# Mamba-2 scan and SwiGLU feed-forward: weight parts by ScalarE and VectorE instead of transfers and GpSimd, and a new step order

## The chip, the core and the metric

The kernel runs on one core of a Trainium2 chip. The core has TensorE (matrix products, "PE" in the profile; its weight loads are "PEld"), VectorE ("DVE"), ScalarE ("ACT"), GpSimd ("POOL") and SyncE ("SP", which here issues nearly all transfers). The metric is device time in microseconds (us), the median of several runs.

## The reference

A scan over the sequence (Mamba-2, in chunks) gives y; y is then the input of a feed-forward block with RMS norm, a gate and a value product, and an output product.

```python
# x (4, 8, 768, 32), a (4, 8, 768), B and C (4, 8, 768, 16), float32
for c in range(768 // 32):
    cum = np.cumsum(np.log(a_c), axis=-1)
    L = np.exp(cum[:, :, :, None] - cum[:, :, None, :]) * causal
    y_intra = ((C_c @ B_c.T) * L) @ x_c
    y_inter = (C_c @ state) * np.exp(cum)
    state = np.exp(cum_last) * state + (B_c * decay_from_j).T @ x_c
x = y.transpose(0, 2, 1, 3).reshape(3072, 256)
xn = x / np.sqrt(np.mean(x * x, -1) + 1e-6) * rms_g
g, v = xn @ w_gate, xn @ w_val        # (256, 1536), float64 inputs
return (g * sigmoid(g) * v) @ w_out   # (1536, 256)
```

## The kernel before

The 3072 tokens are six blocks of 512 (block 0 to 5; the number ahead of the colon in a step's name). The 1536 hidden columns are twelve tiles f of 128, six pairs j of 256. For each block the kernel computes the scan, normalises its output, makes the gate and value products for each f, the SwiGLU, and the output products.

**Weights.** The three weight matrices arrive as 64-bit words and are turned into float32 on the chip, in 20 pieces. Pieces 0 to 13 are gate and value columns (0 to 3 are 128 columns wide, the others 256; even is gate, odd is value; 4 and 5 are pair 1, 6 and 7 pair 2, and so on), pieces 14 to 19 are w_out, two tiles f each. A piece k goes through fetch.k (transfer, SyncE, into one of six buffers "wr"), pow.k, powk.k, powe.k (exponent, three ScalarE instructions, L164, L170, L179), man.k, mane.k (mantissa, VectorE, L186, L194) and wt.k (VectorE, L200).

**Split products.** Six tiles f of block 0 (early, gate) are multiplied in plain float32 straight from the tiles whole_w (columns 0 to 767). All else of gate and value uses a split: every weight tile is cut into a leading part (top, the upper bits), a difference s = ONE * top - w and a trailing part m = w - top, and the normalised input likewise (xm, xs, xl, xh). Step sw.j.k makes top (VectorE, L819) for pair j and k = 0 gate, 1 value; sws.j.k makes s (VectorE, L924); swm.j.k makes m (L929). A product then has three steps: D.f.k (s by xs, L941), W.f.k (ScalarE scales the sum in PSUM, L945), and G.f.k (leading part by xh and trailing part by xl, L952). SiLU is L957 (block 0: silug.f), the product with the value L960 (hidg.f).

**Where the leading parts lie before.** In one tile wgv for all columns. For pairs 0 to 2, step keep.k copies a whole piece from whole_w into wgv by a transfer issued by SyncE (L207); later sw reads it there, and step kt.j.k overwrites it with the top tile, again by a transfer (L934). For pairs 3 to 5 only kt.j.k is needed. The tiles whole_w share their place with the s tiles of pairs 3 to 5.

**Order.** Nothing is scheduled at run time. A list of some 1,530 steps is written out in the code; each step issues its instructions to the engines' queues, and each engine works through its own queue in order. So the list fixes the order on every engine, and a waiting instruction holds up those behind it. Names used below: a, aT, la0 (the decays' start), idle.7 (seven warm-up products), mask, sums, exp (the decay matrices of block 0), L, y.p (scan output of token pair p, 256 tokens), yt.p and sq.p (its copies and squares, ScalarE), 1:S.p (states of the next pair, VectorE), turn (transposes), o.f (output product of block 0), early.f.s (plain products of token half s), gate.f (plain products of all tokens), hid.f (their SwiGLU), a slash and a number (the PSUM pair that a step takes), switch.s (hands PSUM pair s to the split products: s = 1 value, s = 0 gate), rowout and rowe (row sums stored to DRAM).

Of the kernel before, what the change touches and what calls it, by code (L numbers as in the profile page):

```python
# [9 lines left out]
FP32 = mybir.dt.float32  # L10
FP32R = mybir.dt.float32r
# [5 lines left out]
ALU = mybir.AluOpType  # L17
# [4 lines left out]
def kernel(  # L22
# [22 lines left out]
    DM, DF = moe_w_gate.shape  # L45
# [69 lines left out]
    wgv = const.tile([P, 2, 2, DF], FP32R, name="wgv")  # L115
    wgvf = wgv.bitcast(FP32)
    whole_w = [const.tile([P, 2, 2, 256], FP32, tag="sw%d" % (j + NF // 4), name="whole_w")
               for j in range(NF // 4)]

    def whole(n, c, w):  # L120
        return whole_w[c // 256][:, "gv".index(n), :, c % 256:c % 256 + w]
# [82 lines left out]

    def keep(k):
        n, c, w = pieces[k]
        nc.sync.dma_start(out=wgvf[:, "gv".index(n), :, c:c + w], in_=whole(n, c, w))  # L207
# [690 lines left out]
    def split_w(j, k):  # L898
        if j not in Sw:
            if j < NF // 4:  # L900
                Sw[j] = raw.tile([P, 2, 2, 256], FP32R, tag="wr", name="sw", bufs=6)
            else:
                Sw[j] = const.tile([P, 2, 2, 256], FP32R, tag="sw%d" % j, name="sw%d" % j)
# [12 lines left out]
        w = parts.pop((2 + 2 * j + k, "w")) if j >= 3 else wgvf[:, k, :, 256 * j:256 * j + 256]  # L916
# [10 lines left out]
    def trailing_w(j, k):  # L927
        w, s, m = splits[j, k]
        nc.gpsimd.tensor_tensor(out=m, in0=w, in1=tops[j, k], op=ALU.subtract)  # L929
# [3 lines left out]
    def keep_top(j, k):  # L933
        nc.sync.dma_start(out=wgvf[:, k, :, 256 * j:256 * j + 256], in_=tops[j, k])  # L934

    GV = {}
# [11 lines left out]
    def main_gv(blk, f, k):  # L948
        for t in range(2):
            for lhsT, rhs in ((wgv[:, k, t, f * P:(f + 1) * P], xh[blk][:, t]),  # L950
# [180 lines left out]
    def by_vector(out, in_, scale):  # L1131
# [39 lines left out]
        "hidg": lambda f: hide_gv(0, f), "keep": keep, "kt": keep_top,  # L1171
# [15 lines left out]
    def of_chunk(n, fn):  # L1187
# [28 lines left out]
        0:fetch.2 0:set 0:ones 0:zeros 0:upto 0:a 0:ident 0:mid 0:warm 0:whole 0:fetch.0 0:idle.7  # L1216
        0:ident16 0:never 0:whole16 0:mask.0.0/0 0:after 0:bc.0 0:aT 0:bc.1 0:kinks 0:pow.2 0:mids
        0:never16 0:man.2 0:fetch.5 0:after2 0:la0 0:log4.0.4 0:log 0:part 0:part2 0:hmask 0:upto2
        0:mask.1.1/2 0:x.0 0:r.0 0:mean 0:c*2 0:pow.0 0:powk.0 0:tmask 0:mask.0.1/1 0:head 0:sel
        0:turn.0.1 0:parts.0 0:sums.0.1 0:middles 0:turn.0.0 0:cx 0:sums.0.0 0:d 0:exp.0.1 0:T.0.1  # L1220
        0:Tt.0.1.1 0:Tt.0.0.1 0:turn.1.1 0:exp.0.0 0:dx 0:powe.0 0:x.1 0:Tt.0.0.0 0:sums.1.1 0:T.1.1
        0:Tt.1.0.1 0:T.0.0 0:Tt.0.1.0 0:Tt.1.1.1 0:man.0 0:exp.1.1 0:mane.0 0:g.0.1/1 0:turn.1.0
        0:cc 0:scale.1 0:last.1 0:fetch.1 0:Tl.1 0:Tt.1.0.0 0:scale.0 0:L.0.1 0:gcol 0:wt.0
        0:g.0.0/0 0:L.0.0 0:last.0 0:man.5 0:fetch.6 0:mask.1.0/1 0:Tt.1.1.0 0:sums.1.0 0:A.0
        0:powk.2 0:S.0 0:fetch.4 0:row.1 0:T.1.0 0:g.1.0/2 0:A.1 0:Tl.0 0:row.0 0:mane.5 0:g.1.1/0
        0:fetch.9 0:rowout.1 0:pow.5 0:y.0/1 0:mane.2 0:exp.1.0 0:fetch.3 0:L.1.0 0:rowe.1 0:S.1
        0:powk.5 0:L.1.1 0:log4.4.2 0:powe.5 0:wt.5 0:keep.5 0:log4.6.2 0:r.1 0:keep.0 0:powe.2
# [172 lines left out]
```

## Time and profile before

| what | us |
|---|---|
| median of 3 runs | 407.91 |
| lowest and highest | 407.06, 409.32 |
| the profiled execution | 409.15 |
| its span, first to last instruction | 407.4 |
| TensorE busy | 386.8 |
| VectorE busy | 250.2 |
| ScalarE busy | 242.4 |
| GpSimd busy | 59.2 |
| bytes moved by DMA | 31.69 MB |

The mean granted TensorE clock was 0.987 of full speed. "Busy" is the union of an engine's instruction times; a matmul's end is modelled, and a waiting engine counts as idle. A line such as L952 is a line of the kernel's code. In the timeline and the groups, a bracket or the last column gives the idle time just before an instruction and what ended it.

### The profile page before, as it was taken

Reading aid. Unit: us, or ns where it says so; the run is one execution under the profiler, and the core shown is the slowest. Engines: PE = TensorE matmul, PEld = TensorE weight load, DVE = VectorE, ACT = ScalarE, POOL = GpSimd, SP = SyncE. Lnnn points to the kernel's source line nnn. Section 1 sums busy time; section 2 is a strip of 40 time slices with the busy share of each in tenths; the row PEclk is TensorE's granted clock in tenths of the full one; section 3 lists DMA queues with packets and bytes.
Section 4 is the critical chain, followed back from the end, with each engine's and each line's share of the span. In section 5 each row is a group of like instructions: output and inputs, shape, how many; then the busy total and the mean of one; then the engine's idle time right before and its main releaser. Section 6 shows DMA issues by size and latency. Waiting matters only on the chain.

```text
span 407.4 us, 9256 instructions
## 1 busy us (share of the span) xinstructions
PE 386.8 (95%) x3749; PEld 315.5 (77%) x3749; DVE 250.2 (61%) x533; ACT 242.4 (60%) x441; POOL 59.2 (15%) x69
## 2 busy tenths in 40 slices
PE   6999977969999899999999999899999999999997
PEld 4656345648778689987879988689988889988897
DVE  5899989979971447972267643247815158424542
ACT  3899757656768356466773465766575563365530
POOL 3110604123205011120110120101510010000000
PEclk9999998969999999999999999999999999999999
DMA  9967986916561424601343001311000001100001
GB/s 131 251 126 202 244 158 157 257 65 208 126 90 52 67 49 108 73 2 27 108 78 85 32 9 29 101 43 35 0 27 2 2 2 60 51 0 2 0 2 52
DMA packets 98034, 31.69 MB, mean 78 GB/s; under 512 B 77608, under 2 KB 91816, under 8 KB 97992
## 3 DMA queue, kind: packets, MB, share of 16 engines
q1 hardware_dynamic: 93832, 30.85, 33.1%
q10 hardware_dynamic: 4160, 0.26, 0.8%
q8 instruction: 29, 0.48, 0.5%
q14 instruction: 13, 0.11, 0.1%
HBM read 22.64 MB, written 3.74 MB: 65 GB/s over the span
## 4 chain that ended last, share of the span: by engine, by line
PE 70%; DVE 17%; ACT 6%; issue 5%; DMA 2%; SPq 1%; DVEq 0%; ACTq 0%
PE gv L952 26%; PE o L1022 20%; PE gv L941 13%; PE y L703 3%; DVE S L655 2%; PE o L964 2%; DVE m L194 1%; ACT e L164 1%; DVE sw L924 1%; PE g L566 1%; DMA a_sb<-in_a_dram 1%; DVE top L819 1%; DVE m L186 1%; PE tp L509 1%; DVE h L960 1%
## 5 line engine op out<-in xcount | busy, mean ns | idle before, releaser
L952 PE MATMUL gv<-xh,wgv 128*128 128x512 f32 x264 | 108.0, 409 | 0.4 <-ACT gv L945 0.3
L952 PE MATMUL gv<-xl,mw 128*128 128x512 f32 x264 | 104.7, 397 | 0.0
L960 DVE SCALAR_TENSOR_TENSOR h<-gv,u 128x512 f32<-128x512 f32 x66 | 45.4, 690 | 96.3 <-PE gv L952 82.3
L945 ACT ACTIVATE gv<-gv 128x512 f32<-128x512 f32 x132 | 74.9, 587 | 49.3 <-PE gv L941 49.1
L941 PE MATMUL gv<-xs,sw 128*128 128x512 f32 x264 | 81.3, 411 | 6.4 <-DVE sw L924 2.4
L941 PEld LDWEIGHTS gv<-xs,sw 128*128 128x128 f32 x264 | 47.0, 189 | 18.8 <-issue 3.7
L952 PEld LDWEIGHTS gv<-xh,wgv 128*128 128x128 f32 x264 | 50.2, 190 | 12.4 <-ACT gv L945 1.3
L957 ACT ACTIVATE u<-gv 128x512 f32<-128x512 f32 x66 | 39.3, 600 | 32.1 <-PE gv L952 29.0
L952 PEld LDWEIGHTS gv<-xl,mw 128*128 128x128 f32 x264 | 50.3, 191 | 10.2
L479 POOL TENSOR_SCALAR_AFFINE_SELECT L<-L 64x512 f32<-64x512 f32 x32 | 24.4, 763 | 98.8 <-ACT L L477 97.4
L1022 PE MATMUL o<-wo,h 128*128 128x128 f32 x240 | 33.8, 276 | 0.0
L1022 PE MATMUL o<-two,s 128*128 128x128 f32 x240 | 31.9, 276 | 0.8 <-DVE s L995 0.8
L1022 PEld LDWEIGHTS o<-wo,h 128*128 128x128 f32 x240 | 31.2, 191 | 1.7 <-ACT u L957 0.2
L1022 PEld LDWEIGHTS o<-two,s 128*128 128x128 f32 x240 | 29.7, 192 | 1.8 <-DVE s L995 1.2
L1022 PE MATMUL o<-two,h 128*128 128x128 f32 x240 | 30.1, 275 | 0.0
L1022 PEld LDWEIGHTS o<-two,h 128*128 128x128 f32 x240 | 28.6, 192 | 0.2
L1038 ACT COPY v<-o 128x256 f32<-128x256 f32 x15 | 5.6, 372 | 31.6 <-PE o L1022 31.6
L964 PE MATMUL o<-wo,h 128*128 128x256 f32 x96 | 23.2, 392 | 0.2 <-DVE wo L200 0.2
L753 POOL TENSOR_TENSOR sq<-sq,sq 128x512 f32<-128x512 f32 (+1 forms) x6 | 7.0, 1166 | 109.6 <-issue 70.8
L164 ACT ACTIVATE e<-wr,kinks 128x512 int16<-128x512 int16 (+1 forms) x20 | 14.2, 712 | 13.8 <-DMA wgv<-top 5.3
L964 PEld LDWEIGHTS o<-wo,h 128*128 128x128 f32 x96 | 18.8, 198 | 3.5 <-DVE wo L200 0.6
L1022 PEld LDWEIGHTS o<-wo,s 128*128 128x128 f32 x120 | 15.3, 191 | 0.8
(183 smaller groups left out, 547.4 us busy)
## 6 DMA issues: line engine op xcount, KB each, us to landing
L<-rowd SPq DMA_DIRECT2D x32, 128.0 KB, 3.2
xr<-in_x_dram SPq DMA_DIRECT2D x24, 128.0 KB
wgv<-top SPq DMA_DIRECT2D x12, 256.0 KB, 2.5
wr<-in_moe_w_out_dram SPq DMA_DIRECT2D x6, 512.0 KB, 6.5
wr<-in_moe_w_val_dram SPq DMA_DIRECT2D x5, 512.0 KB
wr<-in_moe_w_gate_dram SPq DMA_DIRECT2D x5, 512.0 KB, 4.9
out_dram<-ob SPq DMA_DIRECT2D x9, 256.0 KB, 2.2
br<-in_B_dram SPq DMA_DIRECT2D x22, 64.0 KB, 2.5
```

The costliest lines, as they stand in the source:

```text
L164: nc.scalar.activation(out=k16, in_=words16, func=AF.Relu, scale=1.0 / 16, bias=kinks[:, 0:1])
L479: nc.gpsimd.affine_select(out=L[r], in_=L[r], pattern=[[0, NH], [1, HC]], compare_op=ALU.is_ge, fill=0.0, base=0, channel_multiplier=-1)
L655: nc.vector.scalar_tensor_tensor(out=S, in0=state[2 * g + u - (2 if p < 2 else 1)], scalar=fcol[:, k:k + 1], in1=new[:, u, i], op0=ALU.mul ...
L703: nc.tensor.matmul(out=y[2 * k + u][rows, (2 * n + i) * HC:(2 * n + i + 1) * HC], start=(k, u, rows.start) not in opened, stop=True, skip_ ...
L753: nc.gpsimd.tensor_tensor(out=sqs[blk][:, tk], in0=sqs[blk][:, tk], in1=sq2, op=ALU.add)
L941: nc.tensor.matmul(out=g, lhsT=Sw[f // 2][:, k, t, (f % 2) * P:(f % 2 + 1) * P], rhs=xs[blk][:, t], start=(t == 0), stop=True, skip_group_ ...
L945: nc.scalar.activation(out=GV[f, k], in_=GV[f, k], func=AF.Copy, scale=-BETA * BETA / (BETA + 1.0))
L952: nc.tensor.matmul(out=GV[f, k], lhsT=lhsT, rhs=rhs, start=False, stop=True, skip_group_check=True)
L957: nc.scalar.activation(out=us[f], in_=GV.pop((f, 0)), func=AF.Silu, scale=ONE)
L960: nc.vector.scalar_tensor_tensor(out=hidden_of(blk, f), in0=GV.pop((f, 1)), scalar=ONE, in1=us.pop(f), op0=ALU.mult, op1=ALU.mult)
L964: nc.tensor.matmul(out=o, lhsT=hs_[blk, f // 2][:, f % 2, k // 2, (k % 2) * P:(k % 2 + 1) * P], rhs=wo[:, f], start=opens, stop=(f == NF - ...
L1022: nc.tensor.matmul(out=o[t] if apart else o[:, t * P:(t + 1) * P], lhsT=lhsT[:, t], rhs=rhs, start=(k in (1, 2, 4, 5) and j == 0 and (apar ...
```

## The change

1. The tile wgv is gone. Each pair j and kind k has a leading-part tile of its own, Gw[j, k], and kt.j.k writes it from top with a ScalarE copy.
2. The eight keep transfers are gone. sw reads pairs 0 to 2 from whole_w itself, whose tiles are now one per j and k and share their place with Gw[j, k] instead of with the s tiles of pairs 3 to 5.
3. swm runs on VectorE instead of GpSimd.
4. The list of steps is in another order, on every engine and in every block. Apart from the eight keep steps the two lists hold the same steps.

```diff
@@ -112,13 +112,11 @@
 
     BETA = 4096.0
     ONE = 1.0 + 1.0 / BETA
-    wgv = const.tile([P, 2, 2, DF], FP32R, name="wgv")
-    wgvf = wgv.bitcast(FP32)
-    whole_w = [const.tile([P, 2, 2, 256], FP32, tag="sw%d" % (j + NF // 4), name="whole_w")
-               for j in range(NF // 4)]
+    whole_w = [[const.tile([P, 2, 256], FP32, tag="g%d%d" % (j, k), name="whole_w")
+                for k in range(2)] for j in range(NF // 4)]
 
     def whole(n, c, w):
-        return whole_w[c // 256][:, "gv".index(n), :, c % 256:c % 256 + w]
+        return whole_w[c // 256]["gv".index(n)][:, :, c % 256:c % 256 + w]
 
     wo = const.tile([P, NF, DM], FP32, name="wo")
 
@@ -201,10 +199,6 @@
                                        in1=e, op0=ALU.mult, op1=ALU.mult)
         if dst is None:
             parts[k, "w"] = f
-
-    def keep(k):
-        n, c, w = pieces[k]
-        nc.sync.dma_start(out=wgvf[:, "gv".index(n), :, c:c + w], in_=whole(n, c, w))
 
     a_sb = ffn.tile([BH, S], FP32, tag="ob", name="a_sb", bufs=1)
     lead16 = ffn.tile([P, 16 * P], BF16, tag="h", name="lead16", bufs=NF // 2)
@@ -900,7 +894,7 @@
             if j < NF // 4:
                 Sw[j] = raw.tile([P, 2, 2, 256], FP32R, tag="wr", name="sw", bufs=6)
             else:
-                Sw[j] = const.tile([P, 2, 2, 256], FP32R, tag="sw%d" % j, name="sw%d" % j)
+                Sw[j] = const.tile([P, 2, 2, 256], FP32R, name="sw%d" % j)
         if j in (0, 1):
             if 0 not in Mw:
                 pair = ssd.tile([P, 2, 2, 2, 256], FP32R, tag="L1", name="mw", bufs=1)
@@ -913,7 +907,7 @@
             else:
                 both = const.tile([P, 2, 2, 256], FP32R, name="mw%d" % j)
                 Mw[j] = [both[:, u] for u in range(2)]
-        w = parts.pop((2 + 2 * j + k, "w")) if j >= 3 else wgvf[:, k, :, 256 * j:256 * j + 256]
+        w = parts.pop((2 + 2 * j + k, "w")) if j >= 3 else whole_w[j][k]
         s, m = Sw[j][:, k], Mw[j][k]
         tops[j, k] = top = cvt.tile([P, 2, 256], FP32, tag="e", name="top", bufs=4)
         splits[j, k] = w, s, m
@@ -926,13 +920,15 @@
 
     def trailing_w(j, k):
         w, s, m = splits[j, k]
-        nc.gpsimd.tensor_tensor(out=m, in0=w, in1=tops[j, k], op=ALU.subtract)
+        nc.vector.tensor_tensor(out=m, in0=w, in1=tops[j, k], op=ALU.subtract)
 
     tops, splits = {}, {}
 
-    def keep_top(j, k):
-        nc.sync.dma_start(out=wgvf[:, k, :, 256 * j:256 * j + 256], in_=tops[j, k])
-
+    def rounded_w(j, k):
+        Gw[j, k] = const.tile([P, 2, 256], FP32R, tag="g%d%d" % (j, k), name="gw")
+        nc.scalar.copy(out=Gw[j, k], in_=tops[j, k])
+
+    Gw = {}
     GV = {}
 
     def cross_gv(blk, f, k):
@@ -947,7 +943,7 @@
 
     def main_gv(blk, f, k):
         for t in range(2):
-            for lhsT, rhs in ((wgv[:, k, t, f * P:(f + 1) * P], xh[blk][:, t]),
+            for lhsT, rhs in ((Gw[f // 2, k][:, t, (f % 2) * P:(f % 2 + 1) * P], xh[blk][:, t]),
                               (Mw[f // 2][k][:, t, (f % 2) * P:(f % 2 + 1) * P], xl[blk][:, t])):
                 nc.tensor.matmul(out=GV[f, k], lhsT=lhsT, rhs=rhs, start=False, stop=True,
                                  skip_group_check=True)
@@ -1168,7 +1164,7 @@
         "exps": lambda: ac.preload_act_table_set("natural_log_exp_and_others"),
         "D": lambda f, k: cross_gv(0, f, k), "W": lambda f, k: weigh_gv(0, f, k),
         "G": lambda f, k: main_gv(0, f, k), "silug": lambda f: silu_gv(0, f),
-        "hidg": lambda f: hide_gv(0, f), "keep": keep, "kt": keep_top,
+        "hidg": lambda f: hide_gv(0, f), "kt": rounded_w,
         "row": row_sums, "rowout": row_store, "rowe": row_decays,
         "tok": token_sums, "tokout": lambda: ac.copy(out=tok, in_=ps.pop("tok")),
         "spread": spread, "sub": subtract, "ex": exponential,
```

Of the order, lines that the prediction speaks of. Before:

```diff
-        0:fetch.2 0:set 0:ones 0:zeros 0:upto 0:a 0:ident 0:mid 0:warm 0:whole 0:fetch.0 0:idle.7
-        0:ident16 0:never 0:whole16 0:mask.0.0/0 0:after 0:bc.0 0:aT 0:bc.1 0:kinks 0:pow.2 0:mids
...
-        0:early.1.0/1 0:powk.7 0:norm.0 0:xn.0 0:powe.7 0:keep.2 0:man.7 0:mane.9 0:fetch.8 0:mane.7
...
-        0:powe.10 0:bc.3 0:gate.4/1 0:xs.0.1 0:scale.3 0:pow.12 0:mane.10 0:silu.4 0:y.2/2 0:swm.3.0
-        0:xl.0.0 0:hid.4 0:silu.5 0:xl.0.1 0:ydone.0 0:hid.5 0:xh.0.1 0:sq.2 0:ydone.1 0:kt.3.0
-        0:ydone.2 0:switch.1 0:yt.2 0:kt.3.1 0:D.7.1 0:switch.0 0:fetch.13 0:powk.12 0:D.6.1 0:W.6.1
-        0:bc.5 0:sw.4.1 0:D.6.0 0:wt.10 0:S.3 0:sw.4.0 0:W.6.0 0:swm.4.1 0:D.7.0 0:tok 0:tokout
...
-        0:sw.1.0 0:x.4 0:sws.1.0 0:fetch.16 0:kt.5.1 0:sw.1.1 0:y.3/2 0:W.10.0 0:sq.3 1:S.0 1:S.1
-        0:fetch.18 0:sws.1.1 1:dT.1 0:yt.3 0:swm.1.0 0:G.10.0 0:G.9.1 0:exps 1:turn.0 0:hidg.9
...
```

After:

```diff
+        0:zeros 0:kinks 0:never 0:ident 0:a 0:aT 0:head 0:fetch.5 0:set 0:mean 0:ones 0:after
+        0:after2 0:never16 0:warm 0:ident16 0:upto 0:mid 0:mids 0:bc.0 0:hmask 0:la0 0:upto2
...
+        0:cc 0:wt.5 0:fetch.1 0:mane.0 0:exp.0.1 0:x.1 0:sums.1.1 0:pow.0 0:dx 0:exp.0.0 0:scale.0
+        0:row.1 0:scale.1 0:rowout.1 0:turn.1.1 0:rowe.1 0:T.1.1 0:Tt.1.0.1 0:g.0.1/1 0:L.0.1
...
+        0:x.3 0:xs.0.0 0:xs.0.1 0:mane.10 0:fetch.15 0:gate.5/0 0:S.2 0:hid.4 0:pow.13 0:powk.10
+        0:powk.13 0:silu.5 0:man.11 0:xl.0.0 0:xl.0.1 0:ydone.0 0:hid.5 0:mane.11 0:powe.10 0:wt.10
+        0:fetch.12 0:y.2/2 0:S.3 0:wt.11 0:sq.2 0:ydone.1 0:yt.2 0:sw.4.0 0:ydone.2 0:dT.3
+        0:switch.1 0:D.6.1 0:D.7.1 0:switch.0 0:W.6.1 0:D.6.0 0:D.7.0 0:scale.5 0:x.5 0:W.6.0
+        0:turn.3 0:W.7.0 0:T.3 0:sw.4.1 0:G.6.1 0:Tt.3.0 0:Tt.3.1 0:Td.3 0:G.6.0 0:sws.4.0 1:dT.0
+        0:powe.13 0:W.7.1 0:G.7.0 0:gg.3/2 0:x.4 0:swm.4.0 0:silug.6 0:L1.3.3 0:hidg.6 0:bc.4
+        0:kt.4.1 0:fetch.19 0:D.8.0 0:G.7.1 0:kt.4.0 0:L.3.0 0:D.9.0 0:sws.4.1 0:L1.3.2 0:scale.4
+        0:man.14 0:silug.7 0:hidg.7 0:W.8.0 0:G.8.0 0:pow.14 0:powk.14 0:W.9.0 0:D.8.1 0:powe.14
+        0:y.3/2 0:G.9.0 0:fetch.18 0:swm.4.1 0:pow.12 0:mane.14 0:wt.14 0:D.9.1 0:W.8.1 0:G.8.1
+        0:yt.3 0:sq.3 1:S.0 0:man.15 1:S.1 0:W.9.1 0:man.12 0:silug.8 1:turn.1 0:powk.12 0:pow.15
+        0:powe.12 0:ms.1 0:fetch.17 0:mane.12 0:G.9.1 0:powk.15 0:powe.15 0:wt.12 0:o.0/2 0:o.1
+        0:fetch.16 0:mane.15 0:wt.15 0:o.3 0:hidg.8 0:man.13 0:silug.9 0:sw.5.0 0:rs.1 0:kt.5.0
...
```

## The prediction

> **What bounds the kernel now.** I read the page's first line, then the table of busy time by stretch, because a mean over the span hides stages.
>
> ```profile
> PE 386.8 (95%) x3749; PEld 315.5 (77%) x3749; DVE 250.2 (61%) x533; ACT 242.4 (60%) x441; POOL 59.2 (15%) x69
> ```
>
> The stretches of 60 us (each: length, then busy PE, PEld, DVE, ACT, POOL, then granted clock, DMA share, GB/s):
>
> ```profile
> 0.00:60.00 60.00, 52.86 (x587) 31.82 (x587) 51.56 (x129) 42.71 (x79) 12.80 (x21) 1.00 0.86 187
> 60.00:120.00 60.00, 52.94 (x383) 40.52 (x382) 53.97 (x97) 39.41 (x77) 16.64 (x12) 0.91 0.65 154
> 120.00:180.00 60.00, 58.18 (x703) 50.20 (x702) 35.64 (x78) 36.37 (x67) 12.12 (x17) 1.00 0.34 60
> 180.00:240.00 60.00, 60.00 (x613) 51.60 (x612) 31.35 (x72) 36.83 (x68) 6.62 (x9) 1.00 0.25 58
> ```
>
> From 120 us on TensorE is the bound and the others have a third of their time free. In the first 120 us TensorE is idle 14.2 us, VectorE is busy 105.5 us, and the DMA engines are 86% and 65% busy. What this change can win or lose lies there. The timeline of TensorE names the three large waits (start, duration, then the idle time before and its releaser):
>
> ```profile
> 59.10 1.20 PE L941 MATMUL gv<-xs,sw 128*128 128x512 f32 x4 [2.08 <-DVE h L893]
> 66.96 0.47 PE L941 MATMUL gv<-xs,sw 128*128 128x512 f32 x1 [2.42 <-DVE sw L924]
> 85.90 0.69 PE L509 MATMUL tp<-ident,br 128*128 128x128 f32 x2 [3.46 <-ACT yt L767]
> ```
>
> Behind the second and third the granted clock falls:
>
> ```profile
> 65.00:70.00 5.00, 3.04 (x10) 2.22 (x11) 4.93 (x9) 3.30 (x6) 1.31 (x2) 0.83 0.81 135
> 85.00:90.00 5.00, 4.10 (x19) 2.90 (x20) 4.20 (x11) 4.26 (x9) 0.00 (x0) 0.54 0.12 35
> ```
>
> Narrow windows of that view put it at 0.50 from 68.3 for 3.4 us and from 85.4 for 6.8 us.
>
> Why is VectorE late? The subtraction of L929 is on GpSimd, and VectorE instructions that start under it last until about its end:
>
> ```profile
> L929 POOL TENSOR_TENSOR mw<-wgv,top x6: 1261/1480/1789, 81.9 to 104.8; 128x512 fp32r<-128x512 f32 x6
> ...
> 93.47 1.78 POOL L929 TENSOR_TENSOR mw<-wgv,top 128x512 fp32r<-128x512 f32 x1 [9.05 <-DVE top L819]
> ...
> 92.96 0.42 DVE L819 TENSOR_SCALAR top<-wgv 128x512 int32<-128x512 int32 x1
> 94.03 1.50 DVE L819 TENSOR_SCALAR top<-wgv 128x512 int32<-128x512 int32 x1
> ```
>
> The same instruction takes 0.42 alone and 1.50 beside GpSimd. Last, SyncE's queue and the tile that the change removes:
>
> ```profile
> L934 SPq DMA_DIRECT2D wgv<-top x12: 606/622/657, 52.2 to 108.4; - x12
> L207 SPq DMA_DIRECT2D wgv<-whole_w x8: 593/610/1759, 24.5 to 44.3; - x8
> ...
> 36.92 3.92 SPq L150 DMA_DIRECT2D wr<-in_moe_w_val_dram  x1
> ```
>
> [...]
>
> **The change, part by part.** *Removed transfers:* 8 "keep" (1.5 MB) and 12 "kt" (3 MB), 4.5 of 31.69 MB and 20 x 0.61 = 12 us of SyncE issuing, nearly all before 100 us. No TensorE wait above ends on a DMA, so I credit nothing directly; bounds 0 and -1 (the weights' loads behind them come earlier).
>
> *Copies on ScalarE:* the nearest row is its cast of the same shape (L829, 615 ns): 12 x 0.61 = 7.4 us. ScalarE is busy 39.4 of the 60 us where ten or so of them fall, so their cover is its idle time. Each waits for its top tile, and for tiles 0 to 2 also for the last readers of whole_w, whose place it takes (sws, swm). Behind it on ScalarE stand the next scalings (W) and SiLUs, for which main products and hidden tiles wait. Taken as 0, at most +1, one copy and its wait ahead of a G that follows closely.
>
> *Trailing parts on VectorE:* its subtraction of that shape (L471) lasts 685 ns and follows its neighbour every 0.60 us: 12 x 0.60 to 0.69 = 7.2 to 8.3 us more. What goes away is the stretching. Taking every VectorE instruction that overlaps an L929 against the usual time of its shape: L924 +0.74, L653 +0.66, L492 +1.06, L194 +0.74, L924 +0.99, L655 +0.89 twice, L819 +1.08, L186 +1.09, L840 +0.72, L194 +1.08: 9.9 us. Net -2 us on VectorE, and a trailing part is ready in 0.7 us, not 1.3 to 4.4.
>
> The Trainium skill, "SBUF — State Buffer", says that VectorE and GpSimd arbitrate for a shared pair of ports by an exclusive lock: the loser blocks for the whole instruction. The rows agree: the ends at 95.25 (GpSimd) and 95.53 (VectorE). By that rule the whole 9.9 us goes, as I count it.
>
> *The new order* decides where this lands. For each product I added up the own work queued ahead on TensorE and ahead of its last VectorE producer (each instruction at its usual step, 0.60 for a 128x512 two-input one, stretches left out). The difference is the product's lead. Check on before: the second wait is D.9.0 on sws.4.0, with 57.2 on TensorE and 53.0 on VectorE, lead 4.3. TensorE reached it at 64.55 (7.3 behind its own work), VectorE finished at 66.82 (13.8 behind): 13.8 - 7.3 - 4.3 = 2.2, against 2.4 seen.
>
> (a) Second wait. In the new order the first product on sws.4.0 is D.8.0, lead 5.7. Of VectorE's 13.8 behind, 3.0 were stretches: 10.8 - 7.3 = 3.5 < 5.7, no wait, 2.2 to spare. Take -2.0, bounds -2.4 and 0.
>
> (b) Its half clock: 3.4 us at half speed is 1.7 us of work. Take -1.4, bounds -1.7 and 0.
>
> (c) Third wait: turn waits for yt.3, which stood behind 1:S.0 and 1:S.1, two of whose instructions were stretched by 0.89. In the new order yt.3 and sq.3 come ahead of them, with G.9.0, D.9.1 and G.8.1 queued on TensorE between y.3 and turn. Left is ScalarE's six copies and squares, 2 us, behind 2.8 us of products. Take -2.5, bounds -3.5 and 0.
>
> (d) Its half clock: 6.8 us, 3.4 of work. Take -2.7, bounds -3.4 and 0.
>
> The Trainium skill, "TensorE: Matmul & The Clock Gate", section "HAM oscillation", puts the harm at idle gaps above about 3.4 us. Here a gap of 2.4 us was already followed by 3.4 us at 0.50, so the measurement decides. By the page's number (b) would be 0, since only the third gap is long enough, and the sum would be 1.4 us smaller.
>
> (e) First wait: D.7.1 waited for hid.4, whose SiLU was stuck on ScalarE behind weight steps, with gate.4 the last gate product. In the new order gate.5 is last and hid.4, which frees the bank of D.6.1 and D.7.1, comes earlier. Take -1.5, bounds -2.1 and 0.
>
> (f) Pieces 5 and 6 are converted earlier: 21.8 us of own VectorE work ahead of early.0.0 instead of 19.2, 29.3 instead of 25.5 of ScalarE's ahead of norm.0; leads in this stage drop from 4.3-5.6 to 4.0-4.7. On SyncE fetch.2, fetch.3 and fetch.4 now stand behind rowout.1 and rowe.1, which wait for VectorE and ScalarE; fetch.2 was the first issue of all. What is late next is early.0.0, then early.1.0 (pieces 2 and 3) and gate.2. Take +1.5, bounds 0 and +3.
>
> (g) Start: "a" is issued ahead of the weights, but the warm-up products move behind it:
>
> ```profile
> 2.20 1.68 PE L305 MATMUL idle<-lead 128*128 128x256 bf16 x7 [2.20 <-DVE lead L329]
> 5.63 0.82 PE L310 MATMUL aT<-ident,a_sb 32*128 32x32 f32 x6 [0.91 <-DMA a_sb<-in_a_dram]
> ```
>
> "a" lands up to 1.8 us earlier (fetch.2 no longer ahead), while 1.68 of covered work and a 1.06 mask product lose their cover. Take 0, bounds -1.5 and +1.7.
>
> (h) From 120 us on: same products, same banks, another order; waits there are about 6 us in all with the tail. 0, bounds -2 and +2.
>
> Sum: -2.0 - 1.4 - 2.5 - 2.7 - 1.5 + 1.5 = -8.6. The profiled execution took 409.15 us (span 407.4 plus 1.75 around it): 400.55. It lies 1.24 above the median of 407.91, so the forecast for the median is 399.3, said as 399.5.
>
> **Rivals.** *TensorE never waits in front:* (a) to (e) in full are -13.1; with +1.5 of (f), 396.3, and with the better ends of (f), (g), (h) 391. For it: leads of 8 to 15 us from D.10.0 to 1:D.4.1. Against: six copies still gate turn.
>
> *Given back:* TensorE reaches block 1 early and waits there for weights (kt, swm and sws of tiles 0 to 2 are now just ahead of their use, lead 11 to 15 instead of 12 to 22). The time moves: 404 to 410. Against it: VectorE then lies some 12 behind and TensorE 6 to 7, and 5 to 6 is less than 11.
>
> *Slower: VectorE is the bound at D.8.0.* The subtraction swm.4.0 now stands in VectorE's queue ahead of sws.4.1, swm.4.1 right before G.8.1, with leads of 5.7 to 8. If VectorE there is more than 2.2 us later than I count (from (f), or late weights), TensorE idles again; every 2 us or more also brings a half-clock window. Price: the old waits stay, (f) costs its 3, and the 7.2 of subtractions fall on the path less the 3 of stretches by then: 407.9 + 3 + 4.2 = 415, or 411 with half of it.
>
> **How the numbers follow.** Forecast (394 to 405) 0.55; never waits 0.12; given back 0.13, of which 0.05 lies more than 0.5% below before; slower 0.20. About 0.5%, 2 us, is what a measurement of this kernel can tell from no change. Faster: 0.55 + 0.12 + 0.05 = 0.72; same 0.08; slower 0.20. The range of 8 in 10 leaves out some 0.06 below 392 and 0.10 above 411; the likeliest case alone is 394 to 405.
>
> **What would show it.** VectorE instructions of one shape keep one duration before 110 us (L819 near 0.42, none at 1.5); GpSimd's busy time falls by 20 us to about 38; no wait over 2 us on TensorE after 10 us; clock 1.00 in every 5 us window after that; D.8.0 near 64 to 66 us. Wrong if TensorE's idle time before 120 us stays near 14 us, if a wait on sws.4 or swm.4 is over 2 us, or if waits after 120 us add up to over 9.

## The result, and the profile after

The changed kernel takes 396.12 us (median of 4 runs, 395.49 to 396.62), the kernel before, measured beside it, 407.49. The ratio is 0.9712, 95% interval 0.9676 to 0.9748: faster by 11.4 us. An execution more than 1.5% above the fastest of its kernel is left out of every ratio here; in the experiments this is one of the run with transfers on ScalarE, and one of the kernel before. The profiled execution took 395.73 (span 394.0), 13.4 less than that of before; the latter lay 1.66 above its median and this one 0.39 below. Line numbers have moved by 4 to 6: the mask of top is L813 (was L819), s L918 (L924), the subtraction L923 (L929), D L937 (L941), W L941 (L945), G L948 (L952), turn L503 (L509), the copy of y L761 (L767). L929 is now the ScalarE copy of kt.

First the page's busy times, then the stretches of 60 us in the columns of the prediction:

```profile
PE 379.5 (96%) x3749; PEld 311.2 (79%) x3749; DVE 250.1 (63%) x545; ACT 248.8 (63%) x454; POOL 38.3 (10%) x57
```

```profile
0.00:60.00 60.00, 51.36 (x593) 31.48 (x593) 52.91 (x138) 45.67 (x86) 6.98 (x20) 1.00 0.89 184
60.00:120.00 60.00, 59.31 (x490) 47.17 (x491) 52.35 (x101) 55.00 (x104) 7.50 (x10) 1.00 0.43 84
...
120.00:393.99 273.99, 268.84 (x2668) 232.53 (x2666) 144.81 (x308) 148.15 (x268) 23.82 (x28) 1.00 0.17 40
```

In the first 120 us TensorE is idle 8.64 + 0.69 = 9.3 us instead of 14.2. The second stretch holds 490 products instead of 383. From 120 us to the end TensorE is idle 5.2 us (6.4 before), and has 268.8 us of work left where it had 281.0. VectorE's total is unchanged (250.1 for 250.2) with 12 instructions more.

The timeline of TensorE has these waits of 0.5 us or more in the first 150 us:

```profile
3.20 0.81 PE L304 MATMUL aT<-ident,a_sb 32*128 32x32 f32 x6 [3.20 <-DMA a_sb<-in_a_dram]
10.79 0.33 PE L509 MATMUL tp<-ident,br 128*128 128x128 f32 x1 [1.80 <-ACT early L401]
18.24 0.44 PE L541 MATMUL tp<-ident,Cd 128*128 128x128 f32 x2 [1.18 <-ACT T L1125]
25.25 0.67 PE L355 MATMUL r_ps<-mids,lead 128*128 128x256 f32 x2 [0.56 <-ACT tok L1169]
60.31 0.44 PE L503 MATMUL tp<-ident,br 128*128 128x128 f32 x2 [1.40 <-ACT yt L761]
```

The three waits of before (2.08, 2.42, 3.46) are gone. A new one of 1.40 stands at turn.3, and one of 1.80 at the start. The two windows that had 0.83 and 0.54 of the clock:

```profile
65.00:70.00 5.00, 5.00 (x156) 3.64 (x156) 4.89 (x11) 4.93 (x10) 0.00 (x0) 1.00 0.42 157
...
85.00:90.00 5.00, 4.81 (x21) 3.47 (x21) 5.00 (x11) 4.97 (x10) 0.00 (x0) 1.00 0.74 114
```

The groups of the subtraction, of the mask and of the new copy (shortest, median, longest in ns):

```profile
L923 DVE TENSOR_TENSOR mw<-m,top x6: 680/684/685, 39.0 to 83.6; 128x512 fp32r<-128x512 f32 x6
...
L813 DVE TENSOR_SCALAR top<-whole_w x6: 417/420/426, 86.8 to 104.9; 128x512 int32<-128x512 int32 x6
...
L929 ACT CAST gw<-top x12: 599/617/725, 36.8 to 111.2; 128x512 fp32r<-128x512 f32 x12
```

A subtraction takes 0.68 us on VectorE (1.26 to 1.79 on GpSimd before), a mask keeps its 0.42, the longest 0.43 where it was 1.50. Not every stretch is gone: one of the other six subtractions took 1.13 us, beside a GpSimd selection (L473).

So the 13.4 us of the profiled spans are: 4.9 of idle time before 120 us, 1.2 after it, and 7.3 of busy time. Of the last, 10.2 us at half clock (3.4 and 6.8) account for 5.1. The other 2.2 lie mostly in the first products of block 0 (the 32 score products g<-T went from 4.4 to 2.7 us, the 12 mask products from 4.5 to 3.4). A score product by itself is no shorter (394 ns before, 400 after); they stand in two groups of 16 instead of four of 8. No run here took these 2.2 us apart.

### The profile page after: what moved, and what is told of

Its sections match the earlier page's. It is cut to its first block, busy times and chain, and to the rows that moved or that the text cites. A ratio compares the mean times of both kernels' runs of the same rounds, so it can differ in the third digit from the quotient of the medians.

```text
span 394.0 us, 9186 instructions
## 1 busy us (share of the span) xinstructions
PE 379.5 (96%) x3749; PEld 311.2 (79%) x3749; DVE 250.1 (63%) x545; ACT 248.8 (63%) x454; POOL 38.3 (10%) x57
## 3 DMA queue, kind: packets, MB, share of 16 engines
q1 hardware_dynamic: 88392, 26.13, 30.7%
## 4 chain that ended last, share of the span: by engine, by line
PE 65%; DVE 17%; ACT 7%; SPq 4%; issue 3%; DMA 2%; ACTq 0%; DVEq 0%
PE gv L948 27%; PE o L1018 16%; PE gv L937 14%; PE o L960 4%; PE y L697 3%; DVE m L192 2%; DVE s L994 1%; ACT e L162 1%; SPq L103 1%; DVE xl L834 1%; PE g L560 1%; ACT gv L941 1%; DVE S L649 1%; ACT e L177 1%; SPq L459 1%
## 5 line engine op out<-in xcount | busy, mean ns | idle before, releaser
L948 PE MATMUL gv<-xh,gw 128*128 128x512 f32 x264 | 107.1, 406 | 0.2 <-ACT gv L941 0.2
L948 PE MATMUL gv<-xl,mw 128*128 128x512 f32 x264 | 103.6, 392 | 0.0
L941 ACT ACTIVATE gv<-gv 128x512 f32<-128x512 f32 x132 | 74.7, 588 | 42.6 <-PE gv L937 41.8
L937 PE MATMUL gv<-xs,sw 128*128 128x512 f32 x264 | 79.4, 405 | 1.3 <-DVE xs L828 0.8
L948 PEld LDWEIGHTS gv<-xh,gw 128*128 128x128 f32 x264 | 49.6, 188 | 13.2 <-ACT gv L941 2.0
L937 PEld LDWEIGHTS gv<-xs,sw 128*128 128x128 f32 x264 | 47.3, 188 | 12.9 <-DVE ob L1045 1.1
L948 PEld LDWEIGHTS gv<-xl,mw 128*128 128x128 f32 x264 | 49.7, 188 | 9.6
L473 POOL TENSOR_SCALAR_AFFINE_SELECT L<-L 64x512 f32<-64x512 f32 x32 | 24.8, 775 | 110.3 <-ACT L L471 108.7
L1018 PE MATMUL o<-two,h 128*128 128x128 f32 x240 | 31.0, 276 | 0.2 <-DVE h L988 0.2
L1018 PE MATMUL o<-two,s 128*128 128x128 f32 x240 | 31.1, 275 | 0.0
L960 PE MATMUL o<-wo,h 128*128 128x256 f32 x96 | 21.8, 380 | 0.2 <-DVE wo L198 0.2
L1018 PE MATMUL o<-wo,s 128*128 128x128 f32 x120 | 16.2, 276 | 0.8 <-DVE ob L1045 0.8
```

What stands on the lines that cost most here:

```text
L473: nc.gpsimd.affine_select(out=L[r], in_=L[r], pattern=[[0, NH], [1, HC]], compare_op=ALU.is_ge, fill=0.0, base=0, channel_multiplier=-1)
L937: nc.tensor.matmul(out=g, lhsT=Sw[f // 2][:, k, t, (f % 2) * P:(f % 2 + 1) * P], rhs=xs[blk][:, t], start=(t == 0), stop=True, skip_group_ ...
L941: nc.scalar.activation(out=GV[f, k], in_=GV[f, k], func=AF.Copy, scale=-BETA * BETA / (BETA + 1.0))
L948: nc.tensor.matmul(out=GV[f, k], lhsT=lhsT, rhs=rhs, start=False, stop=True, skip_group_check=True)
L960: nc.tensor.matmul(out=o, lhsT=hs_[blk, f // 2][:, f % 2, k // 2, (k % 2) * P:(k % 2 + 1) * P], rhs=wo[:, f], start=opens, stop=(f == NF - ...
L1018: nc.tensor.matmul(out=o[t] if apart else o[:, t * P:(t + 1) * P], lhsT=lhsT[:, t], rhs=rhs, start=(k in (1, 2, 4, 5) and j == 0 and (apar ...
```

## Experiments

The change has an order and two kinds of operations in it. I ran them apart. Medians in us, and the ratio to the kernel before in the same runs:

| order | copies on ScalarE, no keep | subtraction | us | ratio, 95% |
|---|---|---|---|---|
| before | no | GpSimd | 407.5 | 1 |
| before | no | VectorE | 405.66 | 0.9935 (0.9913 to 0.9957) |
| before | yes | VectorE | 404.67 | 0.9920 (0.9905 to 0.9935) |
| after | no | GpSimd | 427.45 | 1.0478 (1.0462 to 1.0493) |
| after | by transfers, no keep | VectorE | 415.10 | 1.0205 (1.0154 to 1.0257) |
| after | yes | GpSimd | 402.33 | 0.9867 (0.9834 to 0.9899) |
| after | yes | VectorE | 396.12 | 0.9712 (0.9676 to 0.9748) |

The operations in the old order bring 3 us, the new order with the old operations costs 20, both together bring 11. Neither list is quite the other kernel's: one to five steps had to move, as told at the runs. The rest of this section asks why.

### The operations in the old order

```diff
 def trailing_w(j, k):
-    nc.gpsimd.tensor_tensor(out=m, in0=w, in1=tops[j, k], op=ALU.subtract)
+    nc.vector.tensor_tensor(out=m, in0=w, in1=tops[j, k], op=ALU.subtract)
 order: 0:swm.3.0 from behind 0:y.2 to ahead of 0:man.10
```

> The kernel before with one edit: the subtraction of the trailing part on VectorE (and swm.3.0 moved ahead of man.10 to fit the tiles). My theory: the stretches on VectorE go (one 128x512 mask near 0.42, none at 1.5), VectorE's busy time falls by about 2 us, the wait on sws.4.0 becomes about 1.8 and that on yt.3 about 1.7: 402 to 406, and within 1.5 us of the run with all new operations, since the transfers hold nothing. Rival, no shared lock and the 7.2 us of subtractions simply come on top: VectorE +7, 409 to 415. Rival, the transfers matter: this one 3 us or more above the run with all new operations.

And all the changed operations (keep out, kt as a copy, the subtraction on VectorE) in the order of before:

> The kernel before's order of steps with the changed operations: no keep transfers, copies on ScalarE, trailing parts on VectorE. Four steps had to be moved to fit the tiles: swm.3.0 ahead of man.10, kt.3.1 ahead of silu.2, kt.3.0 ahead of silu.4, kt.0.0 ahead of silug.10 and kt.2.0 ahead of pow.19. My theory (both halves needed): ahead of D.9.0 VectorE loses 3.0 us of stretches and gains four subtractions of 0.6, so 13.8 behind becomes 13.2 and the wait on sws.4.0 shrinks from 2.4 to about 1.8; ahead of yt.3 two stretches of 0.89 go, so the 3.46 us wait becomes about 1.7 and its half clock halves or goes: 402 to 406, likeliest 404. Rival, the order is everything: 407.5 within 1.5. Rival, the operations are everything: 395 to 398.

They took 405.66 and 404.67 us. (In the second, five steps were moved; the expectation says four and names all five.) VectorE's busy time fell from 250.2 to 247.7 and 246.9, as the prediction's net of -2 has it. The waits of TensorE in the first of the two runs:

```profile
60.05 2.40 PE L941 MATMUL gv<-xs,sw 128*128 128x512 f32 x8 [3.17 <-DVE h L893]
67.37 0.71 PE L941 MATMUL gv<-xs,sw 128*128 128x512 f32 x2 [1.88 <-DVE sw L924]
83.95 0.44 PE L509 MATMUL tp<-ident,br 128*128 128x128 f32 x2 [1.64 <-ACT yt L767]
```

The second and the third wait came out at 1.88 and 1.64 (1.8 and 1.7 were expected from the stretches taken away and the subtractions put on), and the 6.8 us at half clock behind the third are gone. The first grew here, from 2.08 to 3.17; it is 1.05 in the run with all new operations, which also drops the transfers. That run is 1.0 us faster by the medians, with intervals that overlap and four more steps moved: if this is what the transfers cost in the old order, it is the end of the prediction's bound of 0 to -1. The 10.2 us of half clock fell to 3.4 and 0. "They simply come on top" (409 to 415) is out.

### The order with the old operations

```diff
-        <the kernel before's list>
+        <the changed kernel's list, 0:keep.k behind 0:wt.k for k = 0 to 7,
+         1:x.0 1:x.1 1:spread.0 behind 0:kt.2.1>
```

> The changed kernel's order of steps with the operations of before: keep.0 to keep.7 put right behind their wt, kt as transfers on SyncE, trailing parts on GpSimd. Three issues of SyncE (1:x.0, 1:x.1, 1:spread.0) had to go behind kt.2.1. My theory: the order's leads (5.7 to 8 at D.8.0, yt.3 ahead of 1:S) take away the second and third wait even with the stretches, but a trailing part is ready 1.3 to 4.4 us after its issue and VectorE is 2 to 3 us later: 398 to 402, likeliest 400. Rival, the operations are everything: 406 to 409. Rival, the order is everything: 395.5 to 397.5. Rival, the transfers on SyncE hold the loads of the weights: TensorE waits for a wr tile before 60 us, over 403.

427.45 us: my theory (398 to 402) is wrong, and of the rivals it is, in kind, the one on SyncE's loads (over 403), though no wait of TensorE for a wr tile before 60 us is seen. Three of TensorE's large waits, from the timeline:

```profile
63.84 1.46 PE L703 MATMUL y<-T,S 32*64 32x64 f32 x28 [4.22 <-DVE A L645]
126.79 0.47 PE L952 MATMUL gv<-xh,wgv 128*128 128x512 f32 x1 [3.26 <-DMA wgv<-top]
134.27 5.48 PE L964 MATMUL o<-wo,h 128*128 128x256 f32 x16 [4.42 <-DVE wo L200]
```

The granted clock was 0.964 of full on average, with 30.7 us at 0.50. Behind the first wait VectorE had stood 5.56 us for a load of B, and behind the third 10.56 us for a load of row sums (L<-rowd); both loads stand behind a kt in SyncE's queue. Three issues of later loads were moved in this list; none of the waits shown ends on them, but no run has them moved alone. The next two runs show what the transfers do.

### Transfers in SyncE's queue, and in ScalarE's

```diff
 def rounded_w(j, k):
-    nc.scalar.copy(out=Gw[j, k], in_=tops[j, k])
+    nc.sync.dma_start(out=Gw[j, k].bitcast(FP32), in_=tops[j, k])
```

> The changed kernel with one edit undone: the leading parts go to their tiles (Gw) by a transfer that SyncE issues in the step kt, not by a ScalarE copy; subtractions stay on VectorE, no keep. 1:x.0, 1:x.1 and 1:spread.0 stand behind kt.2.1, since SyncE's queue would lock up otherwise. Theory Q (what costs is the place in SyncE's queue: kt waits there for VectorE, and the loads behind it wait too): bc.5 and bc.3 are issued 5 us or more later than 35.1, a wait of 2 us or more shows up at y.2 or G, 400 to 410. Theory B (bytes and the length of a transfer, no queue): each G that follows its kt closely waits 1 to 2 us, 397 to 400. The record's own term (transfers cost 0 to 1): 396 to 397.

415.10 us (412.25 to 418.05), 19 more than the changed kernel. The trace is of the fastest, 412.25. Here is the chain. SyncE's queue in the changed kernel (the load of bc.5's first part, L103), then the same stretch of the queue with the transfers:

```profile
34.62 0.47 SPq L148 DMA_DIRECT2D wr<-in_moe_w_val_dram  x1
35.13 0.47 SPq L103 DMA_DIRECT2D br<-in_B_dram  x1
```

```profile
36.80 0.58 SPq L148 DMA_DIRECT2D wr<-in_moe_w_val_dram  x1
44.61 0.49 SPq L929 DMA_DIRECT2D gw<-top  x1
45.15 0.58 SPq L103 DMA_DIRECT2D br<-in_B_dram  x1
...
53.78 0.42 DVE L486 TENSOR_TENSOR Bd<-br,d_sb 128x256 f32<-128x256 f32 x1 [4.34 <-DMA br<-in_B_dram]
...
59.30 1.45 PE L697 MATMUL y<-T,S 32*64 32x64 f32 x28 [4.11 <-DVE A L639]
```

SyncE stood from 37.4 to 44.6 at kt.3.0, which waits for VectorE's top. The load behind it went out at 45.15 instead of 35.13. VectorE then waited 4.34 us for that load, the outputs y.2 4.11 for VectorE, and 6.8 us at half clock followed (59.1 to 65.9). Later G.8.0 and 1:G.2.1 wait 1.56 and 2.33 us for the transfer itself, which lands 2.4 us after its issue (median of the 12), and 3.4 us at half clock follow the second. Then comes a second wait by way of the queue: a load of row sums behind kt.1.1 is issued at 117.32 (96.33 in the changed kernel), VectorE stands 8.32 us for it, the output product behind it 2.83 for VectorE's wo, and again 3.4 us run at half clock.

This adds up. By way of the queue: 4.11 and 2.83 of waits, and half of 6.8 and of 3.4 us at half clock, 12.0 us. By the transfer's own length: 1.56 and 2.33, and half of 3.4, 5.6 us. Together 17.6, less the 1.40 at turn.3 that is not there in this run, where the profiled execution is 16.5 longer. No wait of TensorE ends on the three moved loads.

The same transfers issued by ScalarE (`nc.scalar.dma_start` in the same place) leave SyncE's queue as it is:

> As the run before it, but the same transfers are issued by ScalarE where the copies stood, so SyncE's queue is that of the changed kernel. Theory Q: the loads are on time (bc.5 issued near 35), what is left is the longer way of a transfer (some 2 us from issue to landing against a copy of 0.62): within 2 of 396.1, clearly below the run with SyncE. Theory B: about as slow as the run with SyncE.

The three executions that count took 402.63 to 404.61, ratio 0.9894 (0.9852 to 0.9935), which of 407.57 is 403.2. The profile is of the fourth (409.24); I read from it only that bc.5 was issued at 35.20, on time. So of the 19 us some 12 go with the place in SyncE's queue, as theory Q has it, and 7, more than Q's 2, stay with transfers issued by ScalarE. This run leaves the three loads where the changed kernel has them, so the 12 hold their move too. What the 7 consist of was not taken apart here; the 5.6 us above, and ScalarE's 4.2 us of waiting for buffers that a transfer still reads (run with SyncE), are in line with it.

### The subtraction back on GpSimd

```diff
-    nc.vector.tensor_tensor(out=m, in0=w, in1=tops[j, k], op=ALU.subtract)
+    nc.gpsimd.tensor_tensor(out=m, in0=w, in1=tops[j, k], op=ALU.subtract)
```

> The changed kernel with one edit undone: the trailing parts on GpSimd again. My theory: GpSimd's busy time 38 -> 56 to 60, eleven or so VectorE instructions last until the end of a subtraction (1.4 to 1.8 us), VectorE's busy time about 250 -> 252; the margin at D.8.0 (2.2 us by my count) is nearly used up and sub's late result holds a G: 397 to 401, likeliest 398.5. Rival, VectorE has slack everywhere in the new order: within 0.8 of 396.1. Rival, the trailing part on VectorE is the whole gain: over 403.

402.33 us, 6.2 more than the changed kernel: neither "slack everywhere" nor the whole gain, and above the 401 of my theory. First a group, then the timelines of VectorE, GpSimd, ScalarE and TensorE:

```profile
L923 POOL TENSOR_TENSOR mw<-whole_w,top x6: 1262/1664/1801, 94.1 to 116.1; 128x512 fp32r<-128x512 f32 x6
```

```profile
61.91 1.51 DVE L813 TENSOR_SCALAR top<-m 128x512 int32<-128x512 int32 x1
...
111.36 4.67 POOL L473 TENSOR_SCALAR_AFFINE_SELECT L<-L 64x512 f32<-64x512 f32 x6 [5.67 <-ACT L L471]
116.11 1.26 POOL L923 TENSOR_TENSOR mw<-whole_w,top 128x512 fp32r<-128x512 f32 x1
...
117.40 0.62 ACT L929 CAST gw<-top 128x512 fp32r<-128x512 f32 x1 [4.09 <-POOL mw L923]
...
119.38 0.50 PE L948 MATMUL gv<-xh,gw 128*128 128x512 f32 x1 [3.07 <-ACT gv L941]
```

The stretches are back (1.51 for a mask of 0.42; 1.66 for the s of 0.68 behind it), and with them a wait of 0.75 at D.8.0, which the prediction had named as the tight place. VectorE's busy time is 251.4, 1.3 more with 12 subtractions of 0.60 to 0.68 fewer, so the stretches cost 8.5 to 9.5 us (9.9 in the prediction's count). The large wait has another cause, which I had not counted: a subtraction stood on GpSimd behind six selections (4.67 us); the copy into Gw takes the place of whole_w and waits for that subtraction; ScalarE stood 4.09 us at the copy with a W behind it; and G waited 3.07 for W, with 3.4 us at half clock after it. The Trainium skill, "SBUF — State Buffer", has the lock on the shared ports, of which the prediction spoke; here too the row agrees, with 1.51 against 0.42.

### yt.3 and sq.3 late

```diff
-        ... 0:yt.3 0:sq.3 1:S.0 0:man.15 1:S.1 0:W.9.1 ...
+        ... 1:S.0 0:man.15 1:S.1 0:yt.3 0:sq.3 0:W.9.1 ...
```

> The changed kernel with yt.3 and sq.3 put behind 1:S.0 and 1:S.1, where they stood before (term c undone alone). The record's theory: the block turn waits 2 to 3.5 us for yt.3 again and a half-clock window follows: 398.5 to 402. Rival: without stretches and with VectorE 8 us earlier, the four S instructions are done in time, the wait is under 1 us and no half clock follows: 396 to 397.

397.67 us, 1.55 more than the changed kernel. The wait is there, with no window at half clock behind it:

```profile
73.72 0.44 PE L503 MATMUL tp<-ident,br 128*128 128x128 f32 x2 [1.31 <-ACT sq L745]
```

Nearer to the rival. The run undoes more than term (c): in the kernel before only yt.3 stood behind 1:S.0 and 1:S.1, and sq.3 ahead of them (80.43 to 81.15 there), while here sq.3 was moved too and is what the wait ends on. So 1.3 to 1.6 us is the price of both, and at most that of yt.3's place. Of the old wait of 3.46, 1.8 us and the half clock went with the subtraction alone, in the old order (1.64 there).

### How long a wait costs clock

In every profile here in which the granted clock changes, it does so at multiples of 3.41 us of a grid of its own. I cut each of these traces (11, of before and of the experiments, without the one of the transfers on ScalarE) into these cells and added up TensorE's idle time in each. After the first 10 us and ahead of the kernel's end, all 13 cells at full clock with 1.88 us or more of idle time were followed by a cell at 0.50; none with 1.2 us or less was; between these both happened. To test it, the same 18 ScalarE instructions as six waits or as three, in the full stream of products (the edit of the three; the six have six places with 3 each):

```diff
...
         nc.scalar.activation(out=GV[f, k], in_=GV[f, k], func=AF.Copy,
                              scale=-BETA * BETA / (BETA + 1.0))
+        for _ in range({(2, 7, 1): 6, (3, 11, 1): 6, (4, 2, 0): 6}.get((blk, f, k), 0)):
+            nc.scalar.activation(out=GV[f, k], in_=GV[f, k], func=AF.Copy, scale=1.0)
```

> The changed kernel with 18 added ScalarE instructions that scale a product in place by 1.0, three behind each of the steps 2:W.1.0, 2:W.7.1, 3:W.3.0, 3:W.11.1, 4:W.2.0 and 5:W.0.0, so that TensorE waits six times at a full stream of products. Each wait 1.75 less the lead of 0.1 to 0.5: 1.2 to 1.7, 7 to 10 us in all. Clock theory (what counts is the idle share of each 3.41 us cell, and about half of a cell must be idle before the next one runs at 0.50): no half clock, time 396.1 plus the waits, 403 to 406. Rival (every idle gap costs clock): six windows at 0.50, 10 us more.

> The same 18 instructions, six behind each of 2:W.7.1, 3:W.11.1 and 4:W.2.0. Each wait 3.5 less 0.1 to 0.35: about 3.2, 9 to 10 us in all. Clock theory: each is followed by one 3.41 us window at 0.50, that is 1.7 us of work each, 5 us together: 409 to 412, some 5 to 7 above the run with six small gaps. Rival (the clock costs nothing that the waits themselves do not): 405 to 406.5, at most 2 above it.

Six waits (1.21 to 1.48 each, 8.0 in all) gave 405.73 us, three (3.55, 3.26, 3.31, 10.1 in all) 411.10: 5.4 apart where the idle time differs by 2.1. The profiled execution of the six took 404.03, 8.3 more than that of the changed kernel, for 8.0 us of waits. Cells of the second run around each of its waits (length, then busy PE and so on; the clock is the third number from the end):

```profile
190.14:193.55 3.41, 0.54 (x9) 0.16 (x8) 0.96 (x5) 3.25 (x6) 0.00 (x0) 1.00 0.64 134
193.55:196.97 3.42, 2.74 (x7) 2.17 (x8) 0.56 (x1) 1.59 (x4) 0.00 (x0) 0.50 0.02 4
196.97:200.38 3.41, 3.41 (x10) 2.64 (x9) 0.14 (x1) 1.79 (x4) 0.00 (x0) 0.50 0.00 0
272.06:275.47 3.41, 1.11 (x5) 0.94 (x6) 0.06 (x1) 2.15 (x4) 0.58 (x1) 1.00 0.49 134
275.47:278.89 3.42, 3.42 (x18) 3.42 (x17) 2.72 (x6) 0.37 (x1) 0.00 (x0) 0.50 0.00 1
299.36:302.78 3.42, 1.90 (x68) 1.27 (x66) 2.05 (x4) 2.88 (x6) 0.00 (x0) 1.00 0.03 10
302.78:306.19 3.41, 1.62 (x7) 1.36 (x8) 1.04 (x1) 3.33 (x5) 0.00 (x0) 1.00 0.00 0
306.19:309.60 3.41, 3.41 (x17) 2.64 (x16) 0.69 (x1) 3.40 (x6) 0.00 (x0) 1.00 0.00 0
```

The first wait nearly emptied one cell: two cells at half clock. The second left 2.30 us of idle in one cell: one. The third, 3.31 us long, fell across a border, 1.52 and 1.79: none. So the three cells that I expected came by accident, as 2, 1 and 0, and the expected time with them. What counts here is the idle time in a cell and not the length of a wait; the case for it is this third wait, and in the kernel before the wait of 2.08, which fell on two cells as 1.03 and 1.05 with none at half clock behind it. Between 1.3 and 1.8 us the idle time of a cell does not decide it alone, and what else does is open. In the run with six waits no cell of the stream was at half clock.

### Tries at a better version

In the changed kernel ScalarE's cx stood behind its own loads:

```profile
8.77 0.38 ACTq L103 DMA_DIRECT2D br<-in_B_dram  x1
9.80 0.37 ACTq L103 DMA_DIRECT2D cr<-in_C_dram  x1
10.22 0.52 ACT L401 ACTIVATE early<-full_ps 128x416 f32<-128x416 f32 x1 [4.76 <-DMA cr<-in_C_dram]
```

The list with 0:bc.1 moved from ahead of 0:man.5 to behind 0:cx:

> A try at a better version: the changed kernel with 0:bc.1 behind 0:cx, so that ScalarE computes cx (L401) before it issues the two loads whose issues held it from 5.46 to 10.22 us. If ScalarE's held queue is what makes turn.0.0 wait 1.80 us: cx near 8.2, that wait gone, 394 to 395. Rival: the start is bound by what lands (bc.1, fetch.5), the time moves to the next wait (last.1 on ScalarE's T): 395.7 to 396.5.

396.12 us, the same. The 1.80 at the start were gone from the profile, but a wait of 0.48 for bc.1's own load came at 14.15, and 3.4 us at half clock at 19.2. Turn.3 stood at 59.90 instead of 60.31, with its wait of 1.40 as before; these 0.4 us were lost at 153.87, in a wait of 1.02 for VectorE's h that the changed kernel's profile does not have. Then the wait at turn.3. ScalarE's squares of y.2 in the changed kernel, and with 0:S.3 moved from behind 0:y.2 to behind 0:yt.2:

```profile
59.10 0.72 ACT L745 ACTIVATE sq<-y 128x256 f32<-128x256 f32 x3 [2.09 <-DVE S L647]
```

```profile
56.56 0.72 ACT L745 ACTIVATE sq<-y 128x256 f32<-128x256 f32 x3
```

> A try at a better version: the changed kernel with one step moved, 0:S.3 behind 0:yt.2. In the changed kernel ScalarE's squares and copies of y.2 began at 59.10, when VectorE's S.3 had read the same banks (2.09 us of waiting), though y.2 had ended near 56.9; turn.3 then waited 1.40 us for yt.2. If that wait is VectorE's read: ScalarE starts near 57.0, turn.3 waits for nothing, and up to 1.4 us come off: 394.7 to 395.5. Rival, VectorE is late behind it anyway (sws.4.0 ended 0.6 ahead of D.8.0's start): D.8.0 waits instead, 395.7 to 396.3.

394.50 us (ratio 0.9664, 0.9625 to 0.9704). ScalarE starts 2.5 us earlier and TensorE has no wait over 0.3 us from 28 to 156 us. Last, both moves together, and 0:powk.0 0:powe.0 behind 0:Tt.1.1.1:

> The version with 0:S.3 behind 0:yt.2, and two more moves at the start: 0:bc.1 behind 0:cx (turn.0.0 waits 0.5 to 1.8 us for cx) and 0:powk.0 0:powe.0 behind 0:Tt.1.1.1 (last.1 waits 1.18 us, ended by ScalarE's Tt behind those two). In the version with S.3 moved TensorE has no idle gap over 0.3 us from 33.6 to 156. If TensorE is now the bound from 25 us on, 1 to 2 us less at the start come through: 392.5 to 393.7. Rival, VectorE's own queue from 25 to 59 us holds the same time whatever TensorE does before, as in the run with bc.1 alone: 394 to 395.

394.13 us (0.9660, 0.9635 to 0.9684): the rival's number, but not for its reason. The moves at the start had gained nothing by 25 us: with bc.1 behind cx, TensorE waits 1.19 us at 14.98 for that load, and y.0 starts at 22.41 (22.58 in the changed kernel, 22.23 with S.3 moved alone). From there on this profile runs 0.2 us behind that of S.3 alone. The stretch that the rival names, first of the changed kernel, then of this one (length, then busy PE, PEld, DVE, ACT, POOL):

```profile
25.00:60.00 35.00, 33.01 (x388) 19.00 (x388) 34.48 (x77) 29.88 (x54) 2.04 (x3) 1.00 0.88 186
```

```profile
25.00:60.00 35.00, 34.27 (x397) 20.38 (x398) 34.59 (x74) 31.92 (x59) 2.68 (x3) 1.00 0.93 190
```

In this run VectorE is busy 34.6 of the 35 us and TensorE 34.3, with no wait over 0.6 us. Which of the two holds the stretch no run shows. This version is the fastest I have, 2.0 us by the medians below the changed kernel; the intervals of the two ratios overlap at their ends.

## Why the prediction was right, and where it was not

The forecast was 399.5 for a measured 396.12; its working, for the profiled execution, was -8.6 where -13.4 came.

- **Net -2 on VectorE, stretches gone.** Right for the stretches beside a subtraction: the subtraction alone gave -2.5 in the old order, and the mask is at 0.42. In the new order the total stayed (250.1 for 250.2), as more of the stretches beside GpSimd's other work, such as the 1.13, are left: what VectorE's instructions take over the median of their shape, counted from 0.15 us up, is 16.2 us before, 6.2 with the subtraction on VectorE in the old order and 8.9 in the changed kernel.
- **(a), (b): second wait.** Right, and larger: D.8.0 started at 64.57 without a wait, sws.4.0 had ended at 63.96. The margin was 0.6 us, not the 2.2 that I counted; with the subtraction on GpSimd it is a wait of 0.75. Whole worth 2.4 and 1.7.
- **(c), (d): third wait.** Gone whole, 3.5 and 3.4. The mechanism of (c) was half right: putting yt.3 back, with sq.3, costs 1.6 us, and the subtraction alone takes 1.8 us and the half clock away in the old order.
- **(e): first wait.** Gone at D.6.1, which started at 56.79 (59.10 before), but 1.40 us came back behind it at turn.3, where ScalarE waited for VectorE's S.3. I had not looked at who reads y.2's banks ahead of ScalarE.
- **(f): pieces 5 and 6 earlier.** The delay came and went: early.0.0 at 28.45 (+1.7), gate.2 at 39.27 (+1.0), but y.2 at 55.04, 0.2 earlier than before.
- **(g): start.** 0, as taken: aT 2.4 us earlier, then 1.80 lost at turn.0.0; y.0 at 22.58 against 22.53. That its gain would be lost on ScalarE's held queue I had not seen; taking that wait away by itself (bc.1 late) left the time as it was.
- **(h): from 120 us on.** -1.2 of idle time, within its bounds.
- **Copies on ScalarE, 0.** Right; a copy is 0.62 us, and the longest that one made ScalarE wait is 1.4. It was 4.09 with the subtraction on GpSimd.
- **Removed transfers, 0 to -1.** This is the step that failed. Its ground was that no wait of before ends on a transfer. That holds in the old order (1.0 us by medians whose intervals overlap) and says nothing of the new one, where loads stand behind the transfers in SyncE's list: there 19 us hang on it for kt alone, and the order with all old operations is 20 us slower than before. I priced each edit against the old order and summed; but the removal is what makes the new order possible.

The sum was short by 4.8: I took (a) to (e) 3.0 below what they could bring, 3.4 came from places that I had put at nothing, and 1.6 more than I took was lost to other waits. Seen in the two profiles are 8.0 of waits and 5.1 of half clock gone, in full as listed, 3.1 more of other waits in front (1.5 taken), 1.2 less idle time behind 120 us and 2.2 less busy time: 13.4. The number of the rival *TensorE never waits in front*, 396.3, is what was measured, but by luck: TensorE does wait there, 1.80 and 1.40, and the 2.2 of busy time and 1.2 behind 120 us stand in no term of it. *Given back* did not come: from 120 us on TensorE waits less than before. *Slower: VectorE is the bound at D.8.0* was the right place to fear: VectorE is busy 34.5 of the 35 us from 25 to 60 us, and at D.8.0 it was 0.6 us early. That rival's "every 2 us or more also brings a half-clock window" is too simple: the first wait of before, 2.08, brought none.

What the prediction wanted to see was there: GpSimd's busy time 38.3, no wait over 2 us behind 10 us, the clock at 1.00 throughout, D.8.0 between 64 and 66, waits after 120 us of 5.2.

## What to carry to other kernels

Price an order and the operations in it together: an instruction that waits in an in-order queue costs what is queued behind it, so transfers that cost about 1 us in one order can cost 19 us in another. A gain at the start counts only if it is still there later: look for the step at which two profiles meet again (here the gain of two moves at the start was spent by 20 us). And a wait of the matrix engine is priced with the clock behind it: six waits of 1.2 to 1.5 us cost their length here (8.3 for 8.0 us in the profiled execution), and a wait that leaves over half of a 3.41 us cell idle costs some 1.7 us more for each cell at half clock behind it.

## What the runs showed of the hardware

The granted clock is set cell by cell on a 3.41 us grid. The Trainium skill, "TensorE: Matmul & The Clock Gate", Part 1 ("The HAM clock gate"), says that activity is judged in free-running windows of 3413 ns, and the traces agree: every change lies on such a grid, whose phase differs from run to run. The same page's section "HAM oscillation" sets the harm at idle gaps above about 3.4 us; here 1.88 us of idle time in one cell was enough, and a gap of 3.31 across a border did nothing, so the measurement decides. What a half-clock cell at the start costs is open: in the run with bc.1 late an execution with one at 19.2 us took 396.26, and three at full clock 396.01 to 396.13, but another with a mean clock of 0.995 took 397.11.

ScalarE's loads of bc.1 held cx behind them: ScalarE was done with its logarithm by 5.46 us, issued the two at 8.77 and 9.80, and computed at 10.22; with the loads behind it, cx ran at 8.54. An issue stands in its engine's queue like any other instruction, and here one was held for 3.3 us; by what, the profile does not show.
